# A spectral filter's products written class by class, with a new written-out order of all engines

## The chip, the cores and the metric

The kernel runs on one core of a Trainium2 chip. A core has TensorE (PE, matrix products into PSUM), VectorE (DVE), ScalarE (ACT), GpSimd (POOL) and SyncE (SP, which issues most transfers), each with its own queue of instructions that it works off in order, and 16 DMA engines. The metric is the time of one execution on the device, in microseconds.

## The reference

The input x has 2048 rows of 640 bf16 values. It is normalized row by row, and two branches of the normalized rows are added to x: a filter in the frequency domain over both axes, and a bilinear gated unit.

```python
def _A_ref(x, w_r, w_i):
    X = rfft2(x.astype(float32))          # 2048 x 321 complex
    X = X * (w_r + 1j * w_i)
    return irfft2(X, s=(2048, 640)).astype(bfloat16)

def _B_ref(x, w_gate, w_up, w_down):      # 640 x 1536, 640 x 1536, 1536 x 640
    g = x @ w_gate
    u = x @ w_up
    return (g * u) @ w_down

xn = _layernorm(x)
return x + _A_ref(xn, w_r, w_i) + _B_ref(xn, w_gate, w_up, w_down)
```

## The kernel before

The 2048 rows lie as 16 row tiles of 128 rows, `v_x[:, b]`. Everything is cut into named tasks, `T(name, engine, duration, emit, reads, writes, ...)`. A task is a few instructions of one engine. `_PLAN` (line 405) lists all 971 tasks in one written-out order, with the engine of each and its PSUM bank; `replay` (line 151) puts each into its engine's queue in that order, and `compute_waits` (line 196) gives it semaphore waits on the tasks whose buffers or banks it needs. Nothing is decided at run time: an engine that waits holds up everything behind it in its queue. The durations in the code only served to find the order.

The tasks, by name, with the line of their instructions:

- *Normalizing.* bn, ag, sm, sq, sd, rs and mul make statistics and scale the row tile. T0_b (TensorE, line 808) transposes row tile b into PSUM, and eT0_b copies it out: XT, 640 x 2048.
- *Gated unit.* GU_f_b_u (TensorE, line 945) multiplies five chunks of a gate or up matrix by 512 columns of XT. eG copies the result out of PSUM, and H (VectorE, line 985) multiplies gate by up into HT. There are 44 H tasks of 512 elements and six smaller ones.
- *Forward transform.* S1 to S5 (VectorE, lines 851 to 886) are butterflies along the 640 columns, which split the 640 frequencies into five classes by their remainder: four of 64 complex values each, and a fifth, the multiples of five, with 65. R (line 899) transforms along the rows, D (line 1028) finishes the column transform, class by class, with five matmuls of 64 or 65 columns, and eD copies the results to A. C_t (line 1047) finishes the row transform: two matmuls of 321 columns per t, t = 0 to 15, which leave the spectrum in PSUM, real parts on partitions 0 to 63 and imaginary parts on 64 to 127.
- *The filter.* WM_t (VectorE) multiplies this spectrum out of PSUM by w_r and by w_i and writes the products to PR. It has four instructions of 256 elements (line 1064: two weights w, and two halves h of the classes, 32 frequencies each) and a fifth of 260 elements for the class of the multiples of five (line 1067). Two successive t share one PR. SM_t, for odd t (VectorE, lines 1080 and 1081), subtracts and adds the products into the real and imaginary part of the filtered spectrum, L, which has two buffers. JA and JB copy the four classes of L to the other half of the partitions, one of them negated (VectorE or ScalarE), JC and JD do so for the fifth class (GpSimd).
- *Inverse transform.* IA_q (TensorE, line 1110), q = 0 to 31, loads 128 columns of L as weights, once for each class, and multiplies by a table, TI; eIA copies the result to Z2. I (line 1138) transforms along the columns with the table G, V1 to V5 (VectorE, lines 1162 to 1195) are the inverse butterflies.
- *The end.* ACC (TensorE, line 1215) multiplies HT by w_down, and IV (line 1227) adds the last step of the inverse transform into the same PSUM bank. FINA copies it out, FIN (VectorE, line 1254; 1236 for the last tile) adds x, and SyncE stores the tile.

In PR a row of 321 products holds the 65 products of the fifth class, then 256 for the other four, in which the class k runs fastest: four neighbours belong to four classes. L has the same order, so an IA matmul of one class takes its weight columns with a step of four elements (`yl = v_l[:, lr, o_ + 128 + k:o_ + 640:4]`), and those of the fifth class side by side. The PSUM side of a product is read class by class: neighbours in the loop are 64 f32 values apart there, and the filter weights have a step of one or minus one over four elements.

Buffers share memory over time. PR and L lie where US, PQ and F of the forward butterflies were. TI lies where the first tiles of w_down (WD) come later, so the loads of those tiles (ld_wd0 and others, line 676) wait for the IA tasks that read TI. The filter weights come in a ring of three buffers, ld_w0 to ld_w14, each load waiting for the WM tasks that read the buffer last. All these loads stand in SyncE's one queue. `copy_on` (line 680) is the helper of all copies: line 682 on ScalarE, line 683 on VectorE and GpSimd.

Of the kernel before, what the change touches and what calls it, by code (L numbers as in the profile page):

```python
# [255 lines left out]
def _build_tables():  # L256
    t = {}
# [7 lines left out]
    for tt in range(16):  # L265
        for g in range(_G):
            q = tt * _G + g
# [14 lines left out]
    b = np.arange(64)  # L282
# [18 lines left out]
    l_ = 5 * np.arange(65)  # L301
    e = np.exp(-1j * two_pi * ((b[:, None] * l_[None, :]) % _D) / _D)
    w = np.where((l_ == 0) | (l_ == 320), 1.0, 2.0)[:, None] / _D * np.conj(e).T
    for o in range(2):
        own = (l_ % 2 == o).astype(np.float64)
        fd[64 * o:64 * o + 64, 512:577] = e.real * own[None, :]
        fd[64 * o:64 * o + 64, 578:641] = (e.imag * own[None, :])[:, 1:64]
        gd[63:128, 512 + 64 * o:576 + 64 * o] = w.real * own[:, None]
        gd[0:63, 512 + 64 * o:576 + 64 * o] = -(w.imag * own[:, None])[1:64]
# [59 lines left out]
_LP = 321  # L369
_YS = 1090  # L370
# [30 lines left out]
def _d_act(n):  # L401
# [4 lines left out]
    (10, 0, 0), (11, 4, -1), (18, 2, -1), (12, 1, -1), (19, 2, -1), (20, 2, -1), (0, 3, -1), (8, 3, -1), (13, 4, -1),  # L406
    (182, 1, -1), (14, 4, -1), (15, 4, -1), (181, 4, -1), (21, 1, -1), (22, 2, -1), (23, 2, -1), (24, 0, 2), (9, 0, 7),
    (25, 2, -1), (26, 2, -1), (193, 0, 6), (27, 1, -1), (28, 1, -1), (29, 1, -1), (30, 2, -1), (31, 2, -1), (32, 0, 0),
    (43, 1, -1), (44, 1, -1), (183, 4, -1), (36, 2, -1), (34, 2, -1), (33, 2, -1), (35, 2, -1), (45, 1, -1), (46, 2, -1),
    (37, 2, -1), (47, 2, -1), (191, 0, 3), (192, 1, -1), (194, 1, -1), (38, 1, -1), (39, 2, -1), (195, 2, -1), (40, 2, -1),  # L410
    (124, 2, -1), (203, 0, 4), (196, 0, 2), (48, 0, 5), (197, 1, -1), (204, 1, -1), (49, 1, -1), (201, 0, 0), (202, 1, -1),
    (41, 0, 2), (42, 1, -1), (205, 2, -1), (184, 4, -1), (16, 4, -1), (53, 2, -1), (125, 2, -1), (54, 2, -1), (198, 0, 3),
    (199, 1, -1), (200, 2, -1), (64, 1, -1), (55, 2, -1), (50, 2, -1), (51, 2, -1), (208, 0, 1), (209, 1, -1), (206, 0, 7),
    (207, 1, -1), (65, 1, -1), (218, 0, 2), (219, 1, -1), (66, 1, -1), (67, 1, -1), (216, 0, 4), (217, 1, -1), (68, 1, -1),
    (210, 2, -1), (126, 2, -1), (52, 2, -1), (127, 2, -1), (56, 1, -1), (57, 2, -1), (69, 2, -1), (58, 2, -1), (73, 2, -1),
    (70, 2, -1), (128, 2, -1), (211, 0, 3), (212, 1, -1), (213, 0, 0), (214, 1, -1), (215, 2, -1), (186, 4, -1), (223, 0, 5),
    (185, 4, -1), (221, 0, 7), (224, 1, -1), (17, 4, -1), (76, 1, -1), (74, 0, 5), (71, 0, 6), (1, 4, -1), (129, 0, 3),
    (131, 0, 1), (222, 1, -1), (75, 2, -1), (220, 2, -1), (133, 2, -1), (61, 2, -1), (225, 2, -1), (134, 2, -1), (59, 0, 7),
    (72, 1, -1), (77, 1, -1), (132, 1, -1), (130, 1, -1), (78, 1, -1), (60, 2, -1), (135, 2, -1), (226, 0, 5), (227, 1, -1),
    (79, 1, -1), (80, 1, -1), (81, 2, -1), (228, 0, 0), (229, 1, -1), (230, 2, -1), (187, 4, -1), (62, 0, 6), (63, 1, -1),  # L420
    (231, 0, 1), (232, 1, -1), (136, 2, -1), (188, 4, -1), (7, 4, -1), (82, 2, -1), (233, 0, 3), (234, 1, -1), (88, 1, -1),
    (235, 2, -1), (137, 2, -1), (142, 2, -1), (238, 0, 4), (239, 1, -1), (236, 0, 0), (5, 4, -1), (190, 4, -1), (189, 4, -1),
    (241, 0, 1), (237, 1, -1), (89, 1, -1), (240, 2, -1), (85, 2, -1), (138, 0, 2), (139, 1, -1), (243, 0, 5), (244, 1, -1),
    (90, 1, -1), (242, 1, -1), (245, 2, -1), (143, 2, -1), (246, 0, 0), (247, 1, -1), (91, 1, -1), (140, 0, 2), (248, 0, 4),
    (249, 1, -1), (250, 2, -1), (144, 2, -1), (100, 1, -1), (251, 0, 6), (252, 1, -1), (253, 0, 0), (256, 0, 7), (481, 4, -1),
    (258, 0, 4), (92, 1, -1), (101, 1, -1), (141, 1, -1), (254, 1, -1), (257, 1, -1), (102, 1, -1), (255, 2, -1), (145, 2, -1),
    (93, 2, -1), (259, 1, -1), (260, 2, -1), (146, 2, -1), (261, 0, 5), (97, 2, -1), (263, 0, 1), (262, 1, -1), (449, 4, -1),
    (452, 4, -1), (3, 4, -1), (448, 4, -1), (450, 4, -1), (264, 1, -1), (103, 1, -1), (104, 1, -1), (105, 2, -1), (268, 0, 0),
    (269, 1, -1), (265, 2, -1), (106, 2, -1), (94, 2, -1), (155, 2, -1), (273, 0, 3), (151, 0, 4), (274, 1, -1), (152, 1, -1),
    (149, 0, 1), (150, 1, -1), (266, 0, 0), (267, 1, -1), (112, 1, -1), (270, 2, -1), (156, 2, -1), (153, 0, 5), (147, 0, 3),  # L430
    (154, 1, -1), (278, 0, 7), (279, 1, -1), (95, 0, 1), (96, 1, -1), (113, 1, -1), (271, 0, 2), (272, 1, -1), (275, 2, -1),
    (109, 2, -1), (276, 0, 6), (277, 1, -1), (280, 2, -1), (157, 2, -1), (485, 4, -1), (148, 1, -1), (281, 0, 0), (86, 0, 7),
    (114, 1, -1), (282, 1, -1), (283, 0, 2), (284, 1, -1), (115, 1, -1), (116, 1, -1), (285, 2, -1), (117, 2, -1), (158, 2, -1),
    (118, 2, -1), (159, 2, -1), (121, 2, -1), (453, 4, -1), (441, 4, -1), (482, 4, -1), (695, 4, -1), (444, 4, -1), (446, 4, -1),
    (443, 4, -1), (480, 4, -1), (442, 4, -1), (447, 4, -1), (478, 4, -1), (445, 4, -1), (2, 4, -1), (83, 0, 1), (110, 0, 6),
    (98, 0, 5), (291, 0, 3), (292, 1, -1), (84, 1, -1), (87, 1, -1), (111, 1, -1), (288, 0, 0), (289, 1, -1), (286, 0, 2),
    (287, 1, -1), (290, 2, -1), (99, 1, -1), (296, 0, 3), (297, 1, -1), (293, 0, 1), (294, 1, -1), (168, 2, -1), (295, 2, -1),
    (119, 0, 0), (120, 1, -1), (122, 0, 2), (162, 0, 3), (163, 1, -1), (298, 0, 7), (299, 1, -1), (164, 0, 0), (165, 1, -1),
    (166, 0, 5), (167, 1, -1), (303, 0, 4), (107, 0, 0), (300, 2, -1), (169, 2, -1), (451, 4, -1), (454, 4, -1), (304, 1, -1),
    (108, 1, -1), (301, 0, 3), (302, 1, -1), (160, 0, 4), (305, 2, -1), (170, 2, -1), (123, 1, -1), (308, 0, 6), (309, 1, -1),  # L440
    (161, 1, -1), (306, 0, 3), (307, 1, -1), (310, 2, -1), (316, 0, 2), (317, 1, -1), (313, 0, 1), (314, 1, -1), (171, 2, -1),
    (172, 2, -1), (323, 0, 5), (324, 1, -1), (321, 0, 7), (173, 0, 5), (179, 0, 0), (180, 1, -1), (175, 0, 3), (176, 1, -1),
    (322, 2, -1), (311, 0, 2), (174, 2, -1), (177, 0, 0), (509, 4, -1), (513, 4, -1), (4, 4, -1), (484, 4, -1), (312, 2, -1),
    (325, 2, -1), (315, 2, -1), (318, 0, 7), (319, 2, -1), (320, 2, -1), (178, 1, -1), (455, 0, 5), (457, 1, -1), (458, 0, 3),
    (460, 1, -1), (459, 1, -1), (456, 2, -1), (489, 0, 1), (346, 0, 0), (491, 2, -1), (490, 1, -1), (328, 0, 7), (329, 1, -1),
    (347, 1, -1), (461, 0, 4), (462, 2, -1), (333, 0, 3), (334, 1, -1), (463, 0, 6), (486, 0, 1), (487, 1, -1), (488, 1, -1),
    (331, 0, 0), (332, 1, -1), (464, 2, -1), (479, 4, -1), (483, 4, -1), (512, 4, -1), (510, 4, -1), (541, 4, -1), (514, 4, -1),
    (465, 2, -1), (468, 3, -1), (469, 3, -1), (466, 2, -1), (520, 0, 3), (511, 4, -1), (545, 4, -1), (543, 4, -1), (516, 4, -1),
    (522, 1, -1), (521, 1, -1), (326, 0, 5), (327, 1, -1), (330, 2, -1), (467, 2, -1), (335, 2, -1), (336, 0, 7), (337, 1, -1),
    (517, 0, 1), (338, 0, 0), (519, 1, -1), (339, 1, -1), (492, 0, 3), (518, 1, -1), (493, 2, -1), (494, 0, 6), (495, 2, -1),  # L450
    (341, 0, 5), (342, 1, -1), (358, 0, 0), (474, 0, 5), (475, 1, -1), (359, 1, -1), (551, 0, 2), (553, 1, -1), (552, 2, -1),
    (361, 0, 1), (362, 1, -1), (476, 0, 4), (477, 1, -1), (343, 0, 5), (472, 0, 6), (344, 1, -1), (548, 0, 1), (550, 1, -1),
    (470, 0, 3), (549, 1, -1), (471, 1, -1), (353, 0, 0), (496, 2, -1), (473, 2, -1), (542, 4, -1), (515, 4, -1), (523, 0, 5),
    (354, 1, -1), (348, 0, 7), (349, 1, -1), (497, 2, -1), (499, 3, -1), (500, 3, -1), (498, 2, -1), (503, 0, 3), (504, 1, -1),
    (540, 4, -1), (572, 4, -1), (573, 4, -1), (544, 4, -1), (546, 4, -1), (547, 4, -1), (524, 2, -1), (525, 0, 1), (526, 2, -1),
    (340, 2, -1), (574, 4, -1), (527, 2, -1), (345, 2, -1), (576, 4, -1), (608, 4, -1), (607, 4, -1), (605, 4, -1), (501, 0, 0),
    (530, 3, -1), (531, 3, -1), (571, 4, -1), (578, 4, -1), (577, 4, -1), (575, 4, -1), (502, 1, -1), (528, 2, -1), (529, 2, -1),
# [881 lines left out]
```

## Time and profile before

| | us |
|---|---|
| median of three runs | 200.97 |
| lowest and highest | 200.79, 201.59 |
| the profiled execution's own time | 201.59 |
| its span, first to last instruction | 199.8 |
| TensorE busy | 194.2 |
| VectorE busy | 180.6 |
| ScalarE busy | 138.2 |
| GpSimd busy | 12.8 |

The profile is of one execution. A group of instructions is given by its line in the kernel, its engine, its operation, the shapes that it writes and reads, its count, its busy time and the mean time of one in ns, and the idle time of its engine just before it with what ended that. TensorE's weight loads (PEld) run beside its matmuls. Times of one instruction overlap the next one's start on the same engine, so the pace of a series is read from its starts. The chain of work that ended last follows back from the last instruction to what released each one. The granted TensorE clock is 1.00 throughout.

### The profile page before, as it was taken

The page shows a single profiled execution, that of the slowest core. Times are in us where ns is not written, and L with a number is a line of the kernel's source. Part 1 is how long each engine was busy: PE and PEld are TensorE (multiplying, and loading weights), DVE is VectorE, ACT ScalarE, POOL GpSimd, SP SyncE. Part 2 cuts the span into 40 slices and gives each one's busy share as a digit, 9 for nine tenths or more (in the row PEclk, how much of TensorE's full clock was granted, in tenths as well). Part 3 has the DMA queues.
Part 4 walks back from the last instruction along what each step waited for, and adds up shares of the span by engine and source line. Part 5 has one row for each costly group of instructions (what it writes and reads, how often), then busy time and mean ns, then how long its engine had stood idle before and what let it go on. Part 6 is the DMA issues. An engine that isn't in the chain of part 4 may idle for free.

```text
span 199.8 us, 4175 instructions
## 1 busy us (share of the span) xinstructions
PE 194.2 (97%) x1612; PEld 124.3 (62%) x1629; DVE 180.6 (90%) x376; ACT 138.2 (69%) x280; POOL 12.8 (6%) x22
## 2 busy tenths in 40 slices
PE   8899999999999999999999999999999999999995
PEld 8897544455464555555555555557677767777774
DVE  2799999999999889999999999987999999998922
ACT  3899999999997689888898787576205551341230
POOL 1000000000000002122131120220000000000000
PEclk9999999999999999999999999999999999999999
DMA  6999602300079062343153640007002232036332
GB/s 180 330 367 329 215 0 68 79 3 0 0 228 289 13 168 62 91 119 79 38 154 98 152 135 0 0 3 228 7 0 88 73 105 92 16 102 187 98 102 66
DMA packets 21603, 21.78 MB, mean 109 GB/s; under 512 B 2384, under 2 KB 19536, under 8 KB 21456
## 3 DMA queue, kind: packets, MB, share of 16 engines
q1 hardware_dynamic: 20784, 21.11, 36.4%
q10 hardware_dynamic: 800, 0.41, 0.7%
q8 instruction: 13, 0.21, 0.5%
q14 instruction: 6, 0.05, 0.1%
HBM read 18.89 MB, written 2.62 MB: 108 GB/s over the span
## 4 chain that ended last, share of the span: by engine, by line
PE 53%; DVE 26%; ACT 12%; DMA 4%; issue 2%; SPq 2%; DVEq 0%
PE ps L945 23%; PE ps L1215 20%; DVE arena L1064 8%; ACT arena L682 7%; DVE arena L985 4%; DVE arena L683 3%; DVE arena L1081 2%; DVE arena L1080 2%; PE ps L715 2%; ACT arena L737 2%; DMA out_dram<-arena 2%; DVE arena L1067 2%; ACT arena L746 2%; DMA arena<-in_B_w_down_dram 2%; PE ps L899 2%
## 5 line engine op out<-in xcount | busy, mean ns | idle before, releaser
L682 ACT ACTIVATE arena<-ps 128x512 bf16<-128x512 f32 (+6 forms) x219 | 116.4, 590 | 52.4 <-PE ps L1227 19.6
L945 PE MATMUL ps<-arena 128*128 128x512 bf16 x423 | 100.0, 379 | 0.9
L945 PEld LDWEIGHTS ps<-arena 128*128 128x128 bf16 x440 | 40.8, 98 | 41.4
L1215 PE MATMUL ps<-arena 128*128 128x320 bf16 (+2 forms) x396 | 57.0, 295 | 0.8 <-DMA arena<-in_B_w_down_dram 0.4
L1215 PEld LDWEIGHTS ps<-arena 128*128 128x128 bf16 x396 | 37.6, 98 | 14.5 <-issue 0.7
L1064 DVE TENSOR_TENSOR arena<-ps,arena 128x256 bf16<-128x256 f32 x64 | 22.6, 415 | 0.8 <-PE ps L1047 0.7
L985 DVE TENSOR_TENSOR arena<-arena 128x512 bf16<-128x512 bf16 x44 | 18.6, 424 | 0.7 <-ACT arena L682 0.2
L683 DVE CAST arena<-ps 128x512 bf16<-128x512 f32 (+3 forms) x16 | 10.4, 658 | 1.8 <-PE ps L945 1.1
L1254 DVE TENSOR_TENSOR arena<-arena 128x640 bf16<-128x640 bf16 x15 | 7.0, 487 | 5.1 <-ACT arena L682 5.0
L1110 PEld LDWEIGHTS ps<-arena 128*128 128x128 bf16 x160 | 8.1, 117 | 4.0 <-DVE arena L1067 1.3
L746 ACT ACTIVATE arena<-arena 128x640 bf16<-128x640 bf16 x12 | 10.5, 877 | 0.1
L1094 POOL TENSOR_SCALAR arena<-arena 64x252 bf16<-64x252 bf16 x8 | 8.5, 1059 | 30.1 <-DVE arena L1081 29.8
L967 PE MATMUL ps<-arena 128*128 128x128 bf16 (+1 forms) x120 | 9.7, 237 | 0.5 <-DVE arena L683 0.5
L683 POOL COPY arena<-arena 64x252 bf16<-64x252 bf16 x8 | 3.8, 480 | 89.4 <-DVE arena L1081 89.1
L737 ACT ACTIVATE arena<-arena 128x640 bf16<-128x640 bf16 x12 | 9.3, 778 | 0.1
L967 PEld LDWEIGHTS ps<-arena 128*128 128x128 bf16 x120 | 8.4, 98 | 1.3 <-issue 0.6
L1110 PE MATMUL ps<-arena 128*128 128x64 bf16 x160 | 8.8, 198 | 0.0
L1227 PE MATMUL ps<-arena 128*128 128x320 bf16 (+2 forms) x33 | 8.3, 295 | 0.0
L851 DVE TENSOR_TENSOR arena<-arena 128x768 f32<-128x768 bf16 (+1 forms) x10 | 7.9, 793 | 0.1
L1028 PE MATMUL ps<-arena 128*128 128x64 bf16 (+1 forms) x160 | 7.0, 193 | 0.0
L1028 PEld LDWEIGHTS ps<-arena 128*128 128x128 bf16 x160 | 6.2, 98 | 1.3 <-issue 0.2
L1067 DVE TENSOR_TENSOR arena<-ps,arena 128x260 bf16<-128x260 f32 x16 | 6.9, 432 | 0.0
(60 smaller groups left out, 196.0 us busy)
## 6 DMA issues: line engine op xcount, KB each, us to landing
arena<-in_A_x_dram SPq DMA_DIRECT2D x19, 160.0 KB, 3.2
arena<-in_A_w_r_dram SPq DMA_DIRECT2D x30, 80.2 KB, 2.2
arena<-in_A_w_i_dram SPq DMA_DIRECT2D x30, 80.2 KB, 2.2
out_dram<-arena SPq DMA_DIRECT2D x15, 160.0 KB, 1.8
arena<-in_B_w_gate_dram SPq DMA_DIRECT2D x4, 320.0 KB, 6.5
arena<-in_A_x_dram SPq DMA_DIRECT2D x1, 1280.0 KB, 9.6
arena<-c_tf SPq DMA_DIRECT2D x4, 256.0 KB, 4.0
arena<-c_ti SPq DMA_DIRECT2D x2, 512.0 KB, 6.1
```

Source lines behind the costliest of these rows:

```text
L682: return c.e.activation(dst, src, _ACTF.Copy)
L683: return c.e.tensor_copy(dst, src)
L737: return c.e.activation(v_jk, v_x[:, b, :], _ACTF.Copy, scale=1.0 / _D, accum_out=v_m32[:, b:b + 1])
L746: return c.e.activation(v_jk, v_x[:, b, :], _ACTF.Square, scale=-1.0, bias=v_m32[:, b:b + 1], accum_out=v_ss[:, b:b + 1])
L945: ins = c.e.matmul(ps[:, bk, :], v_gw[:, w, j, ft, :], v_xt[:, j, rows], start=(j == 0), stop=(j == 4))
L967: ins = c.e.matmul(ps[:, bk, i * n:(i + 1) * n], v_gw[:, w, j, ft0 + i, :], v_xt[:, j, rows], start=(j == 0), stop=(j == 4))
L985: return c.e.tensor_tensor(v_ht[:, ft0, rows], gb[:, 0, :], gb[:, 1, :], _OP.mult)
L1028: ins = c.e.matmul(ps[:, bk + i, k * 64:k * 64 + n], v_uq[:, k, t + i, :], v_fd[:, k * 128 + w * n: k * 128 + w * n + n], start=True, stop ...
L1064: c.e.tensor_tensor(dst, xh, wv, _OP.mult)
L1067: return c.e.tensor_tensor(d5, x5, wt[:, :, :, 0:321:5], _OP.mult)
L1110: ins = c.e.matmul(ps[:, bk, 64 * k:64 * k + 64], yl, v_ti[:, q, 0, :], start=True, stop=True)
L1215: ins = c.e.matmul(ps[:, bk, 0:sl3.stop - sl3.start], v_ht[:, ft, a * 128:(a + 1) * 128], v_wd[:, ft, sl3], start=(ft == _FT_ORDER[0]), st ...
```

## The change

1. PR and L are laid out class by class. In PR each class takes 66 elements (`_LB`): 64 products and two of padding, or 65 and one for the class of the multiples of five. In L each class takes 128: what SM writes in front and what JA to JD write behind. The loop of a product keeps its order, with the class fastest, so its neighbouring results are now 66 elements apart.
2. SM works on 20 rows of 66 elements in place of four rows of 321. JA to JD take their elements from the new places, in rows of 64 or 63. IA loads 128 neighbouring columns for each class.
3. A new task, pad, sets the two last elements of each class of PR to zero once, on GpSimd, before the first product.
4. The table G has the rows of the fifth class in the new order.
5. `_PLAN` is another written-out order of the now 972 tasks, with other banks, and with some copies on other engines: between WM_0 and SM_15, VectorE has 10 JA and JB tasks (13 before), 15 H (16), 4 eIA (3), no eG (2) and no eD (1). T0_12 stands behind the first D tasks. In SyncE's queue ld_wd0, which waits for IA_8, stands ahead of ld_tf3 and the last fifteen filter loads.

```diff
-        gd[63:128, 512 + 64 * o:576 + 64 * o] = w.real * own[:, None]
-        gd[0:63, 512 + 64 * o:576 + 64 * o] = -(w.imag * own[:, None])[1:64]
+        gd[0:65, 512 + 64 * o:576 + 64 * o] = w.real * own[:, None]
+        gd[65:128, 512 + 64 * o:576 + 64 * o] = -(w.imag * own[:, None])[1:64]
...
+_LB = 66
...
 _PLAN = (
...
-        b_pr = alloc("PR", 8 * 321)
-        b_l = alloc("L", 2 * 2624)
+        b_pr = alloc("PR", 8 * 5 * _LB)
+        b_l = alloc("L", 2 * 2560)
...
-        v_pr = V("PR").rearrange("p (w g n) -> p w g n", w=2, g=4)
-        v_l = V("L").rearrange("p (r n) -> p r n", r=2)
+        v_pr = V("PR").rearrange("p (w g b c) -> p w g b c", w=2, g=4, b=5)
+        v_l = V("L").rearrange("p (r g b c) -> p r g b c", r=2, g=4, b=5)
...
-                        dst = v_pr[:, w, 2 * pb:2 * pb + 2, 65:321].rearrange("p g (h m k) -> p h g m k", h=2, k=4)[:, h]
+                        dst = v_pr[:, w, 2 * pb:2 * pb + 2, 1:5, 32 * h:32 * h + 32].rearrange("p g k m -> p g m k")
                         c.e.tensor_tensor(dst, xh, wv, _OP.mult)
                 x5 = ps[:, bk:bk + 2, 256:321].unsqueeze(1).to_broadcast([128, 2, 2, 65])
-                d5 = v_pr[:, :, 2 * pb:2 * pb + 2, 0:65]
+                d5 = v_pr[:, :, 2 * pb:2 * pb + 2, 0, 0:65]
                 return c.e.tensor_tensor(d5, x5, wt[:, :, :, 0:321:5], _OP.mult)
+            if t == 0:
+                def em_pad(c):
+                    return c.e.memset(v_pr[:].rearrange("p w g b c -> p (w g b) c")[:, :, 64:_LB], 0.0)
+                T("pad", "pool", 300.0, em_pad, writes=[(b_pr, None)], prio=pq - 0.002)
...
             def em_sm(c, lr=lr):
-                pa_, pb_ = v_pr[:, 0], v_pr[:, 1]
-                l_ = v_l[:, lr, 63:2623].rearrange("p (g n) -> p g n", g=4)[:, :, 0:321]
+                pa_, pb_ = (v_pr[:, w].rearrange("p g b c -> p (g b) c") for w in range(2))
+                l_ = v_l[:, lr].rearrange("p g b c -> p (g b) c")[:, :, 0:_LB]
...
-                src = l0[:, :, 1:64] if five else l0[:, :, 65:321]
-                dst = l1[:, :, 0:63] if five else l0[:, :, 321:577]
+                src = v_l[:, lr, :, 0, 1:64] if five else v_l[:, lr, :, 1:5, 0:64]
+                dst = v_l[:, lr, :, 0, 65:128] if five else v_l[:, lr, :, 1:5, 64:128]
...
-                        yl = v_l[:, lr, o_ + 128 + k:o_ + 640:4] if k < 4 else v_l[:, lr, o_:o_ + 128]
+                        yl = v_l[:, lr, q % 4, (k + 1) % 5]
```

## The prediction

> **What bounds the kernel now.** I read first the busy shares and the 40 slices, then the groups by line, then the chain of work that ended last, then the timelines of TensorE and VectorE.
>
> ```profile
> PE 194.2 (97%) x1612; PEld 124.3 (62%) x1629; DVE 180.6 (90%) x376; ACT 138.2 (69%) x280; POOL 12.8 (6%) x22
> PE   8899999999999999999999999999999999999995
> DVE  2799999999999889999999999987999999998922
> PE 53%; DVE 26%; ACT 12%; DMA 4%; issue 2%; SPq 2%; DVEq 0%
> L1064 DVE TENSOR_TENSOR arena<-ps,arena 128x256 bf16<-128x256 f32 x64 | 22.6, 415 | 0.8 <-PE ps L1047 0.7
> L1067 DVE TENSOR_TENSOR arena<-ps,arena 128x260 bf16<-128x260 f32 x16 | 6.9, 432 | 0.0
> L1110 PEld LDWEIGHTS ps<-arena 128*128 128x128 bf16 x160 | 8.1, 117 | 4.0 <-DVE arena L1067 1.3
> L1028 PEld LDWEIGHTS ps<-arena 128*128 128x128 bf16 x160 | 6.2, 98 | 1.3 <-issue 0.2
> ```
>
> TensorE is full, and VectorE has nothing left in slices 14 to 25. Both could set the end, so I ask which waits for which around the changed lines. The chain gives the pace there (start, us, what):
>
> ```profile
> 70.25 0.89 PE ps L1028 x30
> ...
> 102.76 1.33 DVE arena L1064 x4
> 104.09 0.35 DVE arena L1067
> ...
> 122.90 0.82 DVE arena L1080
> 123.74 0.83 DVE arena L1081
> ```
>
> Four products follow each other in 1.33 us, 0.333 us each (the 415 ns above overlap the next one's start); the fifth takes 0.35; an SM pair 1.68. The end of this stage, in the timelines of VectorE, GpSimd and TensorE, and below it the table of stretches for the whole stage (start and end, its length, then busy us of TensorE, weight loads, VectorE, ScalarE, GpSimd, the granted clock):
>
> ```profile
> 130.55 0.82 DVE L1081 TENSOR_TENSOR arena<-arena 64x1284 bf16<-64x1284 bf16 x1
> ...
> 131.46 1.08 POOL L1094 TENSOR_SCALAR arena<-arena 64x252 bf16<-64x252 bf16 x1 [5.13 <-DVE arena L1081]
> 132.59 0.40 POOL L683 COPY arena<-arena 64x252 bf16<-64x252 bf16 x1
> ...
> 129.14 4.48 PE L945 MATMUL ps<-arena 128*128 128x512 bf16 x19
> 133.46 0.84 PE L1110 MATMUL ps<-arena 128*128 128x64 bf16 x20
> 134.13 1.24 PE L945 MATMUL ps<-arena 128*128 128x512 bf16 x5
> ...
> 73.60:131.40 57.80, 57.13 (x498) 31.56 (x505) 56.18 (x131) 48.64 (x90) 10.84 (x14) 1.00 0.32 83
> ```
>
> SM_15 ends at 131.4, GpSimd's two copies at 133.0, and the last four IA tasks start at 133.46 with no idle time before them. From the first product (73.6) to there VectorE works 56.18 of 57.8 us. It has no room: whatever it gets more to do here, TensorE's static order waits for it at the last IA.
>
> **The change part by part.** *Weights of IA now adjacent.* Twenty IA matmuls take 0.67 us (133.46 to 134.13), 33.5 ns each. The D matmuls (L1028), of the same size with adjacent weights, take 0.89 us for 30 in the chain at 70.25, 29.7 ns. So 160 x 3.8 ns = 0.6 us leaves TensorE's queue. This is all the edit can gain there.
>
> *New order and moved tasks.* Between WM_0 and SM_15 VectorE's queue held 16 WM x 1.68 (four at 0.333 and 0.35), 8 SM pairs x 1.68, 13 JA/JB x 0.46, 16 H x 0.43, 2 eG x 0.69, 1 eD 0.83 and 3 eIA x 0.47: 56.8 us; the timeline has 57.8, so 1.0 is waits. Now it holds 16 WM, 8 SM, 10 JA/JB, 15 H and 4 eIA. An SM instruction has 1320 elements for 1284, 36 more at 0.52 ns (512 elements of H in 0.42 us against 1284 of SM in 0.82), 19 ns, so a pair takes 1.72. With WM unchanged that is 26.9 + 13.8 + 4.6 + 6.5 + 1.9 = 53.7, and 54.7 with the same waits. Three more JA/JB on ScalarE cost 3 x 1.05 there; it is idle 9.2 of the 57.8 us, which covers them. If that cover is gone, the IA behind them waits up to 2 us.
>
> Ahead of C_0 TensorE has one more group of five 512-column matmuls (1.08) and one transpose task fewer (0.28), so the stage starts at 74.4. Behind the stage, from the last IA group on, TensorE had 64.0 us to its last matmul (133.46 to 197.5). Now two IA fewer (-0.34) and two groups of five more (+2.16) stand there: 65.8.
>
> *Pad.* One GpSimd memset of 80 elements per partition, after S5_4 and ahead of C_0. The nearest rows are the 1-element memset (0.10 us) and the 252-element copy (0.40 to 0.65). S5_4 ends at 66.6, C_0 starts 73.1: 6.5 us cover it. Behind it on GpSimd stands only JC_1 (78.8); behind C_0, which now waits for it, stand C_1 and the next GLU groups, and WM_0 waits for C_0. Without cover it would cost 0.7 once. JA to JD and the fifth product keep their counts and contiguous rows: nothing. The G table is a constant, its load has the same bytes.
>
> *DMA queue.* SyncE issues the same loads. But ld_wd0 waits for IA_8 and now stands ahead of ld_tf3 and fifteen filter loads that before stood ahead of all such waits. Behind IA_8 come about five issues of 0.45 and a landing of 2.2 to 4 us before WM_10 can run; until then VectorE has WM_9, WM_8, SM_9, a JA and an H, 6 us. Covered, narrowly: 0 taken, 2 us if it isn't.
>
> *The products.* All 64 keep 256 elements, but consecutive results now go 66 elements (132 bytes) apart; before, four went side by side. No row of before writes so. Below: L1064 already reads single f32 elements of PSUM 256 bytes apart, and L1067 reads single bf16 elements 10 bytes apart in SBUF (0.35 us for 260), both at 1.04 ns per element: a hop may be free (0 ns). Nothing can make it a gain, since the rate is already that of a plain copy from PSUM (256 more elements cost 0.27 us between the 128x512 and 128x256 f32 rows: 1.04 ns each). Next: the weight load of L1110, with a step of 4 elements (8 bytes), takes 117 ns for 98, 0.15 ns per element: 38 ns per product. Above: a whole second cycle for each write, 1.04 ns, 0.27 us per product; this is the halving that VectorE's rows show when pairs are lost (1284 bf16 elements at 0.52 ns against 1.04). The step is sixteen times that of L1110, and a write, so I take the middle of those two, 0.6 ns: 0.154 us per product.
>
> A rule of the Trainium skill speaks against this change: "Vector Engine (DVE) Microarchitecture Reference", section "Measured stream behaviour on trn2", says that a port keeps its rate only on runs of two adjacent 4-byte words, and gives 1.71 ns per element for a destination that hops 4 KiB at every element and about 2.5 for a step of 24 words. By these the products' cost, an estimate from that page, would be +11 to +24 us. But read literally it also charges L1067's step of five, where the row shows no loss; it was measured with 32-bit elements, and no row here shows a hopping write.
>
> *Sum.* With p the added time of one product, the last matmul ends at 74.4 + 54.7 + 64p + 2.1 (SM_15's end to IA, as before) + 65.8 = 197.0 + 64p, against 197.5 before. TensorE's own work gives 197.5 - 0.6 = 196.9: both paths meet at p = 0, so every ns of p shows in full. At p = 0.154: -0.5 + 9.9 = +9.4 us. The profiled run took 201.59 (span 199.8 and 1.8 around it), which gives 211.0; it was the slowest of three, 0.62 above their median, on whose scale the forecast is 210.4. VectorE's work behind SM_15 grows by 0.4 us (one H, two eIA, one eG more, two eI fewer); its last V5 ended at 190.0 and the IV that needs it ran at 191.8, which covers that. What is late next: W's ring of loads, which waits for WM, but a slower WM also asks for them later.
>
> **The rivals.** *The hop is free* (the other side): VectorE keeps 0.333 us per product, the stage ends where TensorE arrives, and 0.5 us of the sum remains: 200.5, give or take 1 for waits of the new order. For it: L1064's read side. Against it: L1110. It decides below 8 ns per product for no loss; from 24 ns (1.5 us) on the kernel is slower by more than 0.5%, about what a measurement of this kernel can tell from no change.
>
> *More than a second cycle.* At 1.5 cycles, p is 0.40 and the end +25: 226. For it: nothing in the rows; against it: no row of VectorE shows a third cycle.
>
> *The queue or ScalarE binds.* The hop is nearly free, but the load behind ld_wd0 is late (2 us) or JA and JB on ScalarE delay an IA (up to 2): 202 to 204. Against it: the covers named above.
>
> **How the numbers follow.** Forecast (0.04 to 0.27 us per product) 0.50, its own range 203.0 to 217.7; free 0.20; more than a cycle 0.17; queue or ScalarE 0.13. Of the free case's 0.20, 0.07 are faster by over 0.5%, 0.12 within, 0.01 slower; all else is slower: 0.07, 0.12, 0.81. The range goes from 200.0, under the free case's centre, to 226, the third case's price; a little of the free case and what lies beyond 1.5 cycles are left out.
>
> **What would show it.** The product group at 0.48 us start to start, x64, while the fifth stays at 0.35; SM at 0.84; VectorE busy some 190 us; the IA weight load at 98 ns; TensorE idle some 10 us, in front of IA and C with VectorE's products as releaser, between 75 and 142; SM_15 ending near 139. It is wrong if the products keep 0.333 us, if TensorE waits for a filter load on SyncE, or if the idle time lies behind 142.

## The result, and the profile after

The changed kernel takes 256.83 us (256.16 to 259.01), the one before 200.91 in the same comparison: a ratio of 1.279, 95% interval 1.271 to 1.288. The direction was forecast; the size was not: 210.4 was predicted, and the time lies beyond the range, which ended at 226. The profiled execution has a span of 254.4 us, against 199.8 before.

The page of the changed kernel, shares, slices and the groups that answer to those of before (line 1064 is now 1065, 1067 is 1068, 1110 is 1112):

```profile
PE 209.9 (82%) x1611; PEld 126.8 (50%) x1629; DVE 231.1 (91%) x375; ACT 142.1 (56%) x281; POOL 12.1 (5%) x23
PE   7999999999995737675694857456599999999996
DVE  3899999999989999999979999998969999995872
PEclk9999999999997986889579788979599999999999
PE 60%; DVE 36%; ACT 1%; issue 1%; DMA 1%; ACTq 0%
L1065 DVE TENSOR_TENSOR arena<-ps,arena 128x256 bf16<-128x256 f32 x64 | 75.5, 1462 | 3.8 <-PE ps L1048 3.8
L1068 DVE TENSOR_TENSOR arena<-ps,arena 128x260 bf16<-128x260 f32 x16 | 10.1, 632 | 0.0
L1112 PEld LDWEIGHTS ps<-arena 128*128 128x128 bf16 x160 | 8.1, 105 | 36.1 <-DVE arena L1068 22.7
```

One group above all has grown, from 22.6 to 75.5 us: the 64 products, 415 to 1462 ns each; the fifth products went from 6.9 to 10.1 us. TensorE, full before, now has gaps in slices 13 to 29, all in the stage in which VectorE writes products, and IA waits for the fifth product of a WM task. Outside this stage little moved. The pace, in VectorE's timeline:

```profile
74.37 4.73 DVE L1065 TENSOR_TENSOR arena<-ps,arena 128x256 bf16<-128x256 f32 x4 [0.48 <-PE ps L1048]
78.73 0.63 DVE L1068 TENSOR_TENSOR arena<-ps,arena 128x260 bf16<-128x260 f32 x1
79.28 4.69 DVE L1065 TENSOR_TENSOR arena<-ps,arena 128x256 bf16<-128x256 f32 x4
83.61 0.62 DVE L1068 TENSOR_TENSOR arena<-ps,arena 128x260 bf16<-128x260 f32 x1
84.27 0.84 DVE L1085 TENSOR_TENSOR arena<-arena 64x1320 bf16<-64x1320 bf16 x1
```

Four products take 4.36 us from the first start (74.37) to that of the fifth product (78.73), 1.09 each; it was 0.333. The fifth, whose own work did not change, takes 0.55 instead of 0.35. The end of the stage (the groups of SM's second instruction, with first and last start, then TensorE's timeline), and the table of stretches, with the granted clock behind the busy times:

```profile
L1086 DVE TENSOR_TENSOR arena<-arena x8: 839/840/841, 85.1 to 183.3; 64x1320 bf16<-64x1320 bf16 x8
...
184.85 2.46 PE L946 MATMUL ps<-arena 128*128 128x512 bf16 x10
187.15 0.75 PE L1112 MATMUL ps<-arena 128*128 128x64 bf16 x20
...
74.40:184.10 109.70, 69.98 (x480) 33.25 (x488) 105.23 (x125) 52.13 (x91) 9.99 (x14) 0.82 0.21 53
```

So the 54.6 us of span are found like this. The stage starts 0.8 us later (74.4 for 73.6). From there to the end of SM_15 it takes 109.7 us for 57.8: 64 x 0.757 = 48.4 for the products, 16 x 0.2 = 3.2 for the fifth, 3.1 less for the lighter queue (53.7 + 1.0 waits for 57.8), and 2.9 more idle time of VectorE (109.70 - 105.23 against 57.8 - 56.18): 51.4 of the 51.9. From SM_15 to the last IA tasks it is 3.0 us instead of 2.1, from those to the last matmul 1.0 more.

### The profile page after: what moved, and what is told of

It is laid out like the page before. It is cut to its first block, busy times and chain, and to the rows that moved or that the text cites. A ratio compares the mean times of both kernels' runs of the same rounds, so it can differ in the third digit from the quotient of the medians.

```text
span 254.4 us, 4173 instructions
## 1 busy us (share of the span) xinstructions
PE 209.9 (82%) x1611; PEld 126.8 (50%) x1629; DVE 231.1 (91%) x375; ACT 142.1 (56%) x281; POOL 12.1 (5%) x23
## 4 chain that ended last, share of the span: by engine, by line
PE 60%; DVE 36%; ACT 1%; issue 1%; DMA 1%; ACTq 0%
DVE arena L1065 29%; PE ps L946 27%; PE ps L1217 21%; PE ps L968 3%; PE ps L1140 2%; PE ps L900 2%; PE ps L1229 2%; DVE arena L1068 2%; PE ps L809 2%; DVE arena L986 1%; PE ps L1112 1%; DVE arena L1086 1%; DVE arena L1085 1%; DMA arena<-in_A_x_dram 1%; DVE arena L684 1%
## 5 line engine op out<-in xcount | busy, mean ns | idle before, releaser
L946 PE MATMUL ps<-arena 128*128 128x512 bf16 x422 | 113.3, 414 | 4.0 <-DVE arena L1068 2.7
L1065 DVE TENSOR_TENSOR arena<-ps,arena 128x256 bf16<-128x256 f32 x64 | 75.5, 1462 | 3.8 <-PE ps L1048 3.8
L946 PEld LDWEIGHTS ps<-arena 128*128 128x128 bf16 x440 | 43.1, 104 | 49.8 <-issue 11.4
L1217 PEld LDWEIGHTS ps<-arena 128*128 128x128 bf16 x396 | 37.7, 98 | 13.4
L1112 PE MATMUL ps<-arena 128*128 128x64 bf16 x160 | 10.0, 204 | 27.3 <-DVE arena L1068 18.3
L1112 PEld LDWEIGHTS ps<-arena 128*128 128x128 bf16 x160 | 8.1, 105 | 36.1 <-DVE arena L1068 22.7
L1029 PE MATMUL ps<-arena 128*128 128x64 bf16 (+1 forms) x160 | 8.2, 206 | 8.3 <-DVE arena L1068 8.3
L684 DVE CAST arena<-ps 128x320 bf16<-128x320 f32 (+3 forms) x19 | 11.7, 631 | 2.6 <-PE ps L946 1.1
L1029 PEld LDWEIGHTS ps<-arena 128*128 128x128 bf16 x160 | 7.0, 107 | 12.1 <-DVE arena L1068 7.8
L1068 DVE TENSOR_TENSOR arena<-ps,arena 128x260 bf16<-128x260 f32 x16 | 10.1, 632 | 0.0
L747 ACT ACTIVATE arena<-arena 128x640 bf16<-128x640 bf16 x12 | 10.0, 836 | 0.1
L1097 POOL TENSOR_SCALAR arena<-arena 64x252 bf16<-64x252 bf16 x8 | 7.3, 916 | 52.1 <-DVE arena L1086 51.7
L968 PEld LDWEIGHTS ps<-arena 128*128 128x128 bf16 x120 | 8.4, 98 | 1.4 <-issue 0.7
L738 ACT ACTIVATE arena<-arena 128x640 bf16<-128x640 bf16 x12 | 9.0, 746 | 0.3
L1048 PE MATMUL ps<-arena 128*128 128x321 bf16 x32 | 7.2, 320 | 0.5 <-DVE arena L1086 0.3
```

The source lines that it names most:

```text
L684: return c.e.tensor_copy(dst, src)
L747: return c.e.activation(v_jk, v_x[:, b, :], _ACTF.Square, scale=-1.0, bias=v_m32[:, b:b + 1], accum_out=v_ss[:, b:b + 1])
L946: ins = c.e.matmul(ps[:, bk, :], v_gw[:, w, j, ft, :], v_xt[:, j, rows], start=(j == 0), stop=(j == 4))
L968: ins = c.e.matmul(ps[:, bk, i * n:(i + 1) * n], v_gw[:, w, j, ft0 + i, :], v_xt[:, j, rows], start=(j == 0), stop=(j == 4))
L1029: ins = c.e.matmul(ps[:, bk + i, k * 64:k * 64 + n], v_uq[:, k, t + i, :], v_fd[:, k * 128 + w * n: k * 128 + w * n + n], start=True, stop ...
L1065: c.e.tensor_tensor(dst, xh, wv, _OP.mult)
```

## The experiments

Three theories were set against each other. HOP: all of the loss is the write of a product away from its neighbour. ORDER: the new order of the queues, with ld_wd0 ahead of the filter loads and more copies on ScalarE, has a good part in it. LAYOUT: something else in the new layout costs, such as SM's rows, the pad or the copies. Under HOP it was open what of the write it is: the hop as such, the pitch of 132 bytes, or the two bytes.

### The new order alone

The kernel before takes the new `_PLAN`, with a pad task that clears ten products early; layout and loop stay.

```diff
-_PLAN = ( ... the order of before
+_PLAN = ( ... the new order
...
+            if t == 0:
+                def em_pad(c):
+                    return c.e.memset(v_pr[:, :, :, 0:10], 0.0)
+                T("pad", "pool", 300.0, em_pad, writes=[(b_pr, None)], prio=pq - 0.002)
```

> The kernel before, layout and loop unchanged, with the new order of all engines (the task pad clears ten products that are written later anyway). Theory HOP: the order alone is worth little, 200 to 203 us; products at 0.333 us. Rival ORDER: a good part of the 56 us, 215 or more, with TensorE waiting for filter loads behind ld_wd0 or for copies on ScalarE.

Measured: 200.69 us (200.20 to 201.68, ten runs) against 201.40 of the kernel before on the same chip; ratio 0.996, interval 0.994 to 0.999. The order costs nothing; it gives some 0.4%. The profile puts one wait of TensorE, 0.46 us at 109.6, down to a filter load. This is the fastest kernel of this study that computes what the reference does.

### The new layout alone

The changed kernel takes the order of before, the pad put in behind S5_4.

```diff
-_PLAN = ( ... the new order
+_PLAN = ( ... the order of before, with the pad
```

> The changed kernel, layout, loop and pad as changed, with the order of the kernel before (pad put in behind S5_4). Theory HOP: products at 1.09 us in place of 0.333, so 64 x 0.757 = 48 us and 16 x 0.2 = 3 us for the fifth product more in VectorE's stage: 250 to 258 us. Rival ORDER: clearly less than the changed kernel, 230 or below.

Measured: 256.77 us (255.35 to 258.55 in three runs; a fourth took 261.58), ratio 1.276, interval 1.264 to 1.287. The whole loss comes with layout and loop, and the products' row is the changed kernel's:

```profile
L1065 DVE TENSOR_TENSOR arena<-ps,arena 128x256 bf16<-128x256 f32 x64 | 75.6, 1464 | 2.5 <-PE ps L1048 2.4
```

ORDER falls with these two runs.

### The products put side by side to wrong places

Everything of the change stays, but the products of a class no longer hop: they go, class fastest, to runs of 128 places in PR. The result is not that of the reference; only the write's pattern is taken away.

```diff
-                        dst = v_pr[:, w, 2 * pb:2 * pb + 2, 1:5, 32 * h:32 * h + 32].rearrange("p g k m -> p g m k")
+                        dst = v_pr[:, w, 2 * pb:2 * pb + 2].rearrange("p g b c -> p g (b c)")[:, :, 66 + 132 * h:194 + 132 * h].rearrange("p g (m k) -> p g m k", k=4)
```

> The changed kernel, its layout, order, SM, copies and IA as changed, but the products of a class go side by side to wrong places in PR (runs of 128, class fastest, as before the change), so the output is not the reference's. This takes away the hop alone. Theory HOP: products at 0.333 us, 64 x 0.76 + 16 x 0.2 = 52 us come back, and of the new order's 200.7 the adjacent weights of IA take another 0.6: 200.1, ratio to the kernel before 0.990 to 0.996. Rival LAYOUT (SM's rows of 66, the pad, the copies' rows or the weight loads cost as well): 202 or more.

Measured: 200.16 us (200.06 to 200.89), ratio 0.994, interval 0.992 to 0.996. The 56 us are gone. The groups of the products, the weight loads of IA and the IA matmuls:

```profile
L1065 DVE TENSOR_TENSOR arena<-ps,arena x64: 407/414/426, 74.3 to 126.9; 128x256 bf16<-128x256 f32 x64
L1112 PEld LDWEIGHTS ps<-arena x160: 95/98/101, 82.4 to 131.6; 128*128 128x128 bf16 x160
...
131.07 0.75 PE L1112 MATMUL ps<-arena 128*128 128x64 bf16 x20
```

LAYOUT falls too: SM's longer rows, pad and copies cost nothing that can be measured. The adjacent weights do load in 98 ns instead of 117, and of the last twenty IA matmuls 19 follow at (0.75 - 0.193) / 19 = 29.3 ns, against (0.84 - 0.198) / 19 = 33.8 before. Over 160 that is 0.7 us, and the time is 0.5 below the order alone, which ran on another chip; the intervals of the two ratios overlap, so the rows show this gain better than the times do.

### Half of the products

As the run before, but the products with w_r hop as in the change, and only those with w_i go to wrong places; again the result is not the reference's.

```diff
                         dst = v_pr[:, w, 2 * pb:2 * pb + 2, 1:5, 32 * h:32 * h + 32].rearrange("p g k m -> p g m k")
+                        if w == 1:
+                            dst = v_pr[:, w, 2 * pb:2 * pb + 2].rearrange("p g b c -> p g (b c)")[:, :, 66 + 132 * h:194 + 132 * h].rearrange("p g (m k) -> p g m k", k=4)
```

> As the run before, but only the products with w_i go side by side to wrong places; those with w_r hop as in the changed kernel. The output is not the reference's. Theory HOP, linear from the first ns: 32 x 0.76 = 24 us over the run without hops, the fifth product (which now follows one that does not hop) at 0.35: 223 to 227 us. Rival FOLLOW-ON (part of the 56 us is a consequence that comes only when VectorE is far behind, such as TensorE's lower clock): less than 220.

Measured: 225.80 us (225.79 to 225.81), ratio 1.121, interval 1.118 to 1.124; 25.6 us over the run without hops, 0.80 us for each of the 32 products.

```profile
74.36 3.03 DVE L1067 TENSOR_TENSOR arena<-ps,arena 128x256 bf16<-128x256 f32 x4 [0.48 <-PE ps L1048]
77.31 0.43 DVE L1070 TENSOR_TENSOR arena<-ps,arena 128x260 bf16<-128x260 f32 x1
...
74.40:154.00 79.60, 55.55 (x479) 28.00 (x487) 78.39 (x124) 51.56 (x91) 9.99 (x14) 1.00 0.30 73
```

Four products, two of each kind, take 2.95 us. The extra time does not fall on the hopping products alone. In this first task the trace has 1304 ns for the first product, which stands behind an idle engine; 1521 for the second, behind a hopping one; 628 for the third, which does not hop but follows one that does; and 408 for the fourth. A hopping product thus leaves some 0.2 us to the instruction behind it. The fifth, now behind a product that doesn't hop, starts its successor 0.35 later, as before the change (77.31 to 77.66); its extra 0.2 us in the changed kernel was the tail of the hopping product in front of it. Counted with its tail, a hopping product costs (2.95 - 4 x 0.333) / 2 = 0.81 us here and (4 x 0.757 + 0.2) / 4 = 0.81 in the changed kernel: VectorE's time shows in the end in full.

By that each half of the products is worth 32 x 0.81 = 25.8 us. The second half costs 256.83 - 225.80 = 31.0, by the spans 254.4 - 224.1 = 30.3. The rest is time in which the engines wait for each other: in its stage VectorE is idle for 4.5 us in the changed kernel (109.70 - 105.23) and for 1.2 here (79.60 - 78.39), and from the end of SM_15 to the last IA tasks it is 3.0 us there and 1.7 here. The last section shows where that comes from. FOLLOW-ON, which gave less than 220 here, falls as a main cause; this part of it is real.

### The loop turned round

The changed kernel with frequency fastest and class outside: results lie side by side, the filter weights are read 10 elements (20 bytes) apart. It computes what the reference does.

```diff
-                        xh = ps[:, bk:bk + 2, 0:256].rearrange("p g (k h m) -> p h g m k", k=4, h=2)[:, h]
-                        wv = wt[:, w, :, 0:320].rearrange("p g (m k) -> p g m k", k=10)
-                        wv = wv[:, :, :, 1:5] if h == 0 else wv[:, :, :, 9:5:-1]
-                        dst = v_pr[:, w, 2 * pb:2 * pb + 2, 1:5, 32 * h:32 * h + 32].rearrange("p g k m -> p g m k")
+                        xh = ps[:, bk:bk + 2, 0:256].rearrange("p g (k h m) -> p h g k m", k=4, h=2)[:, h]
+                        wv = wt[:, w, :, 0:320].rearrange("p g (m k) -> p g k m", k=10)
+                        wv = wv[:, :, 1:5] if h == 0 else wv[:, :, 9:5:-1]
+                        dst = v_pr[:, w, 2 * pb:2 * pb + 2, 1:5, 32 * h:32 * h + 32]
```

> The changed kernel with the loop of a product turned round: frequency fastest, class outside, so that results lie side by side in rows of 32, the spectrum is read side by side out of PSUM, and the filter weights are read 10 elements (20 bytes) apart. Nothing else differs. Theory HOP: only the write side costs; products back at 0.333 us start to start, stage back to some 55 us, 200 to 203 us in all. Rival READ: a read that hops 20 bytes costs as the write did; products stay near 1.1 us and the time near 250. Rival ORDER (the new order is what costs): 220 us or more with products at 0.333.

Measured: 212.40 us (212.32 to 212.64), ratio 1.055, interval 1.051 to 1.058. Neither 200 nor 250:

```profile
74.40 2.19 DVE L1065 TENSOR_TENSOR arena<-ps,arena 128x256 bf16<-128x256 f32 x4 [0.47 <-PE ps L1048]
76.51 0.44 DVE L1068 TENSOR_TENSOR arena<-ps,arena 128x260 bf16<-128x260 f32 x1
```

A product takes 2.11 / 4 = 0.53 us, 0.195 more than before. 64 x 0.195 = 12.5, and the run without hops plus that is 212.7. So a read that hops 20 bytes costs too, but a quarter of what the write does. HOP as I had put it for this run ("only the write side costs") is wrong in that.

### What of the write it is: two lists of single products

Neither is the filter kernel. Each instruction stands alone, so the figures are durations, and the order of before takes 424 ns here for the kernel's 415. A hopping product takes 1294 - 424 = 870 ns more, against 0.81 us in the kernel; the lists show what the price depends on, and the kernel what it is there.

> Not the filter kernel: a list of single VectorE products of 256 elements, each alone (every one waits for the one before), four of each pattern, then copies on ScalarE; its output is not the reference's. Each line changes one thing: the pitch of the classes in the result (32 to 2048 elements), f32 in place of bf16 results, sources in PSUM or SBUF, one step throughout (1 to 80), runs of 2, 4 and 8 results, the other order of the loop, and reads that hop. Theory HOP (every result written away from its neighbour costs the same three cycles): all pitches from 32 up take about 1.1 to 1.5 us, the interleaved order 0.41. Rival BANK (it is the pitch of 66, 132 bytes): the time depends on the pitch and is much lower at some, up to 0.41 at the best. Rival HALFWORD (a 2-byte write of its own is what costs): f32 results at the same byte pitch come near 0.41. Rival READ (the sources' hops count as well): sources side by side, with the result 66 apart, take clearly less than with both hopping.

The lines that decide (line 52 is the order of before; then class pitches of 32, 66, 80 and 2048 elements; f32 results at a pitch of 132 bytes; sources side by side in SBUF with a result pitch of 66; a plain copy on VectorE from sources side by side in SBUF, pitch 66; the turned loop; on ScalarE a copy in the order of before and one with pitch 66):

```profile
L52 DVE TENSOR_TENSOR o<-ps,s 128x256 bf16<-128x256 f32 x4 | 1.7, 424 | 0.1
L53 DVE TENSOR_TENSOR o<-ps,s 128x256 bf16<-128x256 f32 x4 | 5.1, 1267 | 0.1
L60 DVE TENSOR_TENSOR o<-ps,s 128x256 bf16<-128x256 f32 x4 | 5.2, 1294 | 0.1
L63 DVE TENSOR_TENSOR o<-ps,s 128x256 bf16<-128x256 f32 x4 | 4.9, 1232 | 0.1
L67 DVE TENSOR_TENSOR o<-ps,s 128x256 bf16<-128x256 f32 x4 | 5.2, 1293 | 0.1
L69 DVE TENSOR_TENSOR o<-ps,s 128x256 f32<-128x256 f32 x4 | 2.4, 598 | 0.1
L73 DVE TENSOR_TENSOR o<-s 128x256 bf16<-128x256 bf16 x4 | 5.2, 1293 | 0.1
L75 DVE COPY o<-s 128x256 bf16<-128x256 bf16 x4 | 3.0, 740 | 0.1
L96 DVE TENSOR_TENSOR o<-ps,s 128x256 bf16<-128x256 f32 x4 | 2.4, 605 | 0.1
L116 ACT ACTIVATE oa<-ps 128x256 bf16<-128x256 f32 x4 | 1.5, 383 | 189.1 <-DVE o L99 189.0
L118 ACT ACTIVATE oa<-ps 128x256 bf16<-128x256 f32 x4 | 5.2, 1304 | 0.1
```

BANK falls: all pitches from 32 to 2048 elements lie between 1.23 and 1.30 us, but for 1.43 at 96. READ falls as the cause: with sources side by side it is 1.29 still. HALFWORD is half right: an f32 result at the same byte pitch takes 598 ns, not 1294, but not 415 either. ScalarE pays the same as VectorE. One form pays less: a plain copy from bf16 values side by side in SBUF takes 740 ns at the same pitch, where the cast out of PSUM takes 1292; why, no run shows. A rule of the Trainium skill, "Vector Engine (DVE) Microarchitecture Reference", section "Measured stream behaviour on trn2", gives 1.71 ns per 32-bit element for a hopping destination; the f32 row gives 1.04 + (598 - 424) / 256 = 1.72. It agrees, for the elements that it was measured with; the page's 2.5 for a step of 24 words was not seen here, at hops of 33 words. For bf16 results it is (1294 - 158) / 256 = 4.4 ns, with 158 = 424 - 256 x 1.04, which no figure there covers.

> Again single VectorE products of 256 elements, each alone, then weight loads on TensorE with their columns 1, 2, 4, 8 and 16 elements apart; its output is not the reference's. Theory LINE (a bf16 result costs 4.4 ns for every visit to a new 16-byte line, worked out from the first probe: (1290 - 158) / 256 at a step of 8, (726 - 158) / 128 at 4): steps 3, 6, 7 and 9 take 580, 1000, 1140 and 1290 ns, 1 and 2 some 430; runs of 2 results 720, runs of 4 440. Rival WORD (only a result that leaves half of a 4-byte word unwritten costs): runs of 2 that fill a word come at 430 to 600, and the same runs one element further on, which fill no word, at 1290. f32 results at steps 2 and more: 600. Reads: up to 5 elements 430 (as the fifth product's in the kernel), from 8 on 610. Weight loads: 98 ns at 1, 117 at 4, more at 8 and 16.

The second list, results out of PSUM with one step throughout: 2, 3, 4, 6, 7 and 9 elements.

```profile
L54 DVE TENSOR_TENSOR o<-ps,s 128x256 bf16<-128x256 f32 x4 | 1.8, 444 | 0.1
L55 DVE TENSOR_TENSOR o<-ps,s 128x256 bf16<-128x256 f32 x4 | 2.3, 584 | 0.1
L56 DVE TENSOR_TENSOR o<-ps,s 128x256 bf16<-128x256 f32 x4 | 2.9, 724 | 0.1
L57 DVE TENSOR_TENSOR o<-ps,s 128x256 bf16<-128x256 f32 x4 | 4.0, 1007 | 0.1
L58 DVE TENSOR_TENSOR o<-ps,s 128x256 bf16<-128x256 f32 x4 | 4.6, 1149 | 0.1
L59 DVE TENSOR_TENSOR o<-ps,s 128x256 bf16<-128x256 f32 x4 | 5.1, 1274 | 0.1
```

LINE gave 580, 1000, 1140 and 1290 for steps 3, 6, 7 and 9: within 16 ns. But it also gave 720 for runs of two results 66 apart. Those (at 69.2 us), and the same runs one element further on (at 71.0):

```profile
L71 DVE TENSOR_TENSOR o<-ps,s x1: 424/424/424, 69.2 to 69.2; 128x256 bf16<-128x256 f32 x1
...
L71 DVE TENSOR_TENSOR o<-ps,s x1: 867/867/867, 71.0 to 71.0; 128x256 bf16<-128x256 f32 x1
```

A pair that fills a 4-byte word is free, though it hops 132 bytes; so are runs of 4, 8 and 32 (424 to 426 ns). The same pair across two words costs 867, where WORD gave 1290. Both theories are needed: bf16 results of a product that leave half a word unwritten cost 4.4 ns for each visit to a 16-byte line. The odd pairs fit that without a new number: they stand 132 bytes apart, every fourth crosses into a second line, so 128 runs make 160 visits, and 160 x 4.4 + 158 = 862. Why half a word costs so much was not shown.

Full words are not free either, they are cheaper. With the f32 row's 1.72 ns for a visit, f32 results 3 and 4 words apart come to 192 x 1.72 + 158 = 488 and 598 ns; measured are 495 and 607. Out of PSUM the pairs' 128 visits (378 ns) hide behind the plain 424. With both sources side by side in SBUF, where plain results take 292 ns, they don't:

```profile
L89 DVE TENSOR_TENSOR o<-s 128x256 bf16<-128x256 bf16 x4 | 1.5, 385 | 0.1
```

Reads go by the same 1.72. With filter weights 2, 4, 5, 6, 8, 10 and 66 elements apart a product takes 424, 424, 429, 485, 599, 604 and 602 ns; by line visits that would be 378 ns for 4 elements, hidden behind the 424, then 433 for 5, 488 for 6 and 598 from 8 on.

```profile
L81 DVE TENSOR_TENSOR o<-ps,s 128x256 bf16<-128x256 f32 x4 | 1.7, 429 | 0.1
L84 DVE TENSOR_TENSOR o<-ps,s 128x256 bf16<-128x256 f32 x4 | 2.4, 604 | 0.1
```

So the fifth product's step of five (10 bytes) is the last of those tried that is all but free, and 20 bytes cost 604 - 424 = 180 ns, near the turned loop's 195. The weight loads in this list ran while TensorE's pace was changing (the same loads with step 1 took 127 ns at its start and 100 at its end), so they decide nothing.

## Why the prediction was wrong

- *IA's adjacent weights, 0.6 us*: right, 0.5 by the times and 0.7 by the rows.
- *The new order, the DMA queue, the copies on ScalarE, the pad*: costed at nothing, and right; the order even gives 0.7 us. The rival of a late load behind ld_wd0 did not occur: the changed kernel has no wait of TensorE for a filter load, the order alone one of 0.46 us.
- *Every ns of p shows in full*: right, and it is what let a single group move the end by a quarter. The sum 197.0 + 64p, with the measured p = 0.757 and the fifth's 3.2 us, gives 248.6 for the last matmul; it ended at 252.1. The 3.5 missing are mostly VectorE's idle time of 2.9 and the last IA tasks' delay of 0.9. The sum took TensorE's pace as given; the last section shows that it was not.
- *The fifth product at 0.35*: wrong by 0.2 us each. I had looked at its own pattern and not at what the instruction in front of it leaves running.
- *The size of p*: this is the step that failed. The sum had 0.154 us for the added time of one product, and it measured 0.757. "Above: a whole second cycle for each write, 1.04 ns" was no bound. It came from rows with results side by side (0.52 against 1.04 ns), and nothing in the trace of before wrote an element alone. The measured price is 2.96 ns per element in the kernel, 2.8 cycles of 1.04 ns. Taking the middle of 0.15 and 1.04 ns then made a forecast of a number that had no row at all. The rival "more than a second cycle" had the right direction and stopped at 1.5 for the same reason ("no row of VectorE shows a third cycle"). With p at 0.757 the same sum would have given some 249 us, and 252 with the fifth's 3.2, for the measured 256.8.
- *The page's estimate, +11 to +24 us*: nearer, and still under half. The reservation in the prediction, that it was measured with 32-bit elements, was the one that mattered, but I read it as a reason for less instead of more.
- *The reason for "the hop may be free"*: L1064's hopping reads out of PSUM are free (424 ns in the lists, with the hop and without), and so is L1067's step of 10 bytes (429). Neither says anything of a write.

## What to carry to other kernels

Look at the write side of a VectorE or ScalarE instruction first: 256 bf16 results that do not fill 4-byte words in succession took 1230 to 1430 ns for 424 or less, at any step of 8 elements or more that was tried (a plain copy inside SBUF 740), while pairs that fill words hopped for free out of PSUM, and so did reads out of PSUM. When a rearrangement has to hop somewhere, put it on the PSUM read, here the loop of before did; the step that it left in the weight columns of the next stage cost only 4.5 ns per matmul (33.8 for 29.3). And where the trace has no row like the new operation, a neighbouring row is not an upper bound; a range then has to be wide, or one instruction measured by itself.

## What was not expected of the hardware

The granted TensorE clock fell from 1.00 to 0.82 over the stage, as TensorE waited. It is 0.50 in eight spells and 1.00 between them. The longest is 120.3 to 130.6 us, where five matmuls of 512 columns that take 1.08 us elsewhere took 2.15.

```profile
120.00:130.00 10.00, 7.65 (x50) 3.37 (x47) 9.14 (x13) 4.66 (x8) 1.22 (x2) 0.51 0.15 35
125.40 2.15 PE ps L946 x5
```

This is where the second half's extra time comes from. Behind four of the spells VectorE waits for C's matmuls: 0.43 us at 101.4, 1.36 at 130.7, 0.50 at 144.2 and 1.01 at 172.5, 3.3 together. In the run with half of the products hopping the only such wait is that of the very first product, 0.48 us, which the changed kernel has too. In the last spell, 178.4 to 185.2, five matmuls ahead of the last IA tasks take 2.11 us instead of 1.08. So VectorE's delay made TensorE wait, and a slower TensorE then delayed VectorE again, by some 4.5 us in all, an estimate from these rows; a run that keeps the clock up was not made.

The Trainium skill, "TensorE: Matmul & The Clock Gate", section "Part 1: The HAM clock gate (the "warmup" mystery)", says that the clock halves after an idle window of about 3.4 us. The spells here last 3.4, 6.8 or 10.3 us, which agrees with a window of that length. The waits of the matmuls ahead of them were only 2.4 to 3.1 us, and behind the longest, 3.2 us up to 163.2, the clock stayed at 1.00, so the length of a wait alone does not decide it here. In the run with half of the products hopping, where no wait of the matmuls in the stage was over 2.0 us, the clock stayed at 1.00.

Not tried was a loop over pairs of neighbouring frequencies, which would fill words and hop, but needs one dimension more in the result's pattern, and would still read the weights 20 bytes apart.
